# x's first two blocks in halves on both DMA queues, the gate weights on GpSimd's queue, and one warming product less, in a gated pair of linear-attention blocks

## The chip, the cores and the metric

The kernel runs on one core of a Trainium2 chip. The metric is the device time of one execution in microseconds (us); lower is better. A run gives one such time, and a kernel is judged by the median of its runs. One execution was also taken by the hardware profiler; its page and trace give times from the start of the span, in us unless marked ns.

The engines are TensorE (PE for its matrix products, PEld for its weight loads), VectorE (DVE), ScalarE (ACT), GpSimd (POOL) and SyncE (SP). A transfer is issued by an engine's queue (SPq, ACTq); the data are moved by 16 DMA engines that all queues share.

## What is computed

Two linear-attention blocks, A and B, work on the same x (2048 rows of 640, bf16) with weights of their own, and a sigmoid gate mixes them:

```
g = sigmoid((x * gate_w).sum(-1))
q, k, v = split of x @ wqkv, 32 heads of 20
phi(t) = where(t > 0, t + 1, exp(t)) + 1e-6
kv = sum over rows of phi(k) v^T;  z = sum over rows of phi(k)
o = phi(q) kv / (phi(q) z + 1e-6);  a = o @ wo
out = g * a_A + (1 - g) * a_B
```

A_x alone is used as x; B_x is not read.

## The kernel before

Everything stays in SBUF for the whole run. The contraction over 640 is done in five slices of 128 (DT = 5), the 2048 rows in 16 chunks of 128 (ST = 16), four chunks to a stretch of 512 (NB = 4, CB = 4). xT holds x transposed, xn holds it as it is; wk, wq and wv hold the slices of the weights.

*The loads of the start* (lines 151 to 173). The first 512 rows of x come as four blocks of 128 rows (load_x, line 152: 128 partitions of 1280 bytes, 160 KB; block q holds every fourth row). SP's queue issues block 0, slice 0 of A's key weights (load_wk, line 155, 160 KB), the gate weights g5 (line 161, five rows of 256 bytes), slice 2 of the key weights and slices 3 and 4 in one. ACT's queue issues block 1, slice 1 of the key weights, block 2, block 3, and then loads ACT's table of functions (line 165). After that SP issues A's query weights in three transfers (line 169) and 15 transposing loads (line 172), which bring the other three stretches of 512 rows into xT, five slices to a stretch. The framework gives the transfers of these two queues semaphores in turn, and a transfer that reuses one waits for the transfer that had it.

*GpSimd* builds constants: the identity `ident` (two instructions from masks.py, needed by the transpositions below), then maskE, I4, spread, E4 and an fp32 identity, which are read later.

*Warming products* (lines 208 and 209). Before x is there TensorE multiplies constants: six products of 512 columns and one of 256, whose result is not read.

*The first products* (k_first, lines 316 to 341, in an order written out by hand). x_transpose (lines 247 to 253) transposes a block of x by five TensorE products with the identity into PSUM, and VectorE copies them to xT in two pieces. gate_column (lines 220 to 225) transposes the gate weights in the same way, and ACT copies them as column 641 behind the key weights, so that the product for the second half of k (321 columns instead of 320) also yields the gate's sum. The order on TensorE is: the transpositions of blocks 0 and 1; the gate's transposition; eight products of k for blocks 0 and 1 with slices 0 and 1 (line 295, first the halves of 320 columns, then those of 321); the transpositions of block 2; four products with slice 2; the transpositions of block 3; the rest of k for blocks 0 to 3. After that come q for the first 512 rows, k for chunks 4 to 7 (these read the transposing loads' first stretch), and so on.

*The rest* (from line 947, an order written out by hand inside `tc.manual_schedule()`). k and q of both blocks, the sums over rows and the products with wv and wo follow, many of them in Strassen's form, with PSUM banks handed on from stage to stage. At lines 959 to 962 SP issues three loads, which bring the other three stretches of x into xn (640 KB each); A's wv and wo follow on the same queue. The first reader of these rows of xn is x_sum on VectorE (line 698).

Of the kernel before, what the change touches and what calls it, by code (L numbers as in the profile page):

```python
# [9 lines left out]
P = 128  # L10
# [9 lines left out]
NB = 4  # L20
CB = 4
HB = 512
# [6 lines left out]
RB = 256  # L29
# [4 lines left out]
def kernel(  # L34
# [11 lines left out]
    nc = tc.nc  # L46
    x2 = A_x.flatten_outer_dims()
# [44 lines left out]
    xn = persist.tile([P, ST, D], BF16, name="xn")  # L92
# [17 lines left out]
    g5 = persist.tile([DT, P], BF16, name="g5")  # L110
# [35 lines left out]
    xb0 = x2[0:CB * P, :].rearrange("(p q) d -> p q d", q=CB)  # L146
# [4 lines left out]
    def load_x(eng, lo, hi):  # L151
        eng.dma_start(out=xn[:, lo:hi, :], in_=xb0[:, lo:hi, :])

    def load_wk(eng, lo, hi):
        eng.dma_start(out=wk[0][:, lo:hi, 0:D], in_=wq_dram[0][:, lo:hi, D:2 * D])

    load_x(nc.sync, 0, 1)
    load_x(nc.scalar, 1, 2)
    load_wk(nc.sync, 0, 1)
    load_wk(nc.scalar, 1, 2)  # L160
    nc.sync.dma_start(out=g5[:], in_=gate_w.rearrange("(c p) -> c p", p=P))
    load_x(nc.scalar, 2, 3)
    load_wk(nc.sync, 2, 3)
    load_x(nc.scalar, 3, 4)
# [5 lines left out]
    for n in range(1, NB):  # L170
        for c in range(DT):
            nc.sync.dma_start_transpose(
                out=xT[:, c, n * HB:(n + 1) * HB], in_=x2[n * HB:(n + 1) * HB, c * P:(c + 1) * P]
# [4 lines left out]
    for r in range(4):  # L178
        rows = slice(32 * r, 32 * r + 32)
        nc.gpsimd.tensor_copy(out=I4[rows], in_=ident[rows, rows])  # L180
    nc.gpsimd.tensor_copy(
        out=spread[:].rearrange("p (h t) -> p h t", t=TW), in_=I4[:, :, None].to_broadcast([P, H, TW])
    )
    nc.gpsimd.memset(maskE[:], 1.0)
    for lo in range(0, HF, K6):
        part = maskE[:, lo:min(lo + K6, HF)]
        for sign, base in ((1, 0), (-1, Dh - 1)):
            nc.gpsimd.affine_select(
                out=part, in_=part, pattern=[[-sign * Dh, part.shape[1] // Dh], [0, Dh]],
# [3 lines left out]
    for rows, n in ((slice(0, 2 * H), H // 2), (slice(2 * H, P), H)):  # L193
        nc.gpsimd.tensor_copy(
            out=E4_rows[rows, 0:n], in_=I4[rows, 0:n, None].to_broadcast([rows.stop - rows.start, n, Dh])
# [9 lines left out]
    warm_raw = ps_raw("warm", 0)  # L205
    warm = banks(warm_raw)
    one_l, one_r = [nc.const_aps.tensor(1.0, [P, n], BF16) for n in (P, HB)]
    for n in [HB] * 6 + [RB]:
        nc.tensor.matmul(warm[:, 0, 0:n], lhsT=one_l, rhs=one_r[:, 0:n], start=True, stop=True)

    def by_group(dst, lhsT, src):
# [97 lines left out]
    def k_chunk(b, i, slot=None, lifted=False, between=None):  # L309
        pt = ps(f"k{'AB'[b]}", slot)  # L310
        for hf in range(2):
            for c in range(DT):
                k_mm(b, i, c, pt, hf)
        k_done(b, i, pt, lifted, between)
# [632 lines left out]
    with tc.manual_schedule():  # L947
# [8 lines left out]
        early = [(lambda k: lambda: sq_sum(k, 1))(k) for k in range(2, 5)] + [None, None]  # L956
        for i in range(hc, ST - 3):
            k_chunk(0, i, None, i in (8, 9, 11, 12), early[i - hc])
        for n in range(1, NB):
            nc.sync.dma_start(  # L960
                out=xn[:, n * CB:(n + 1) * CB, :], in_=x2[n * HB:(n + 1) * HB, :].rearrange("(q p) d -> p q d", p=P)
            )
        wv[0] = load_w(0, "v", nc.sync)
        load_wo(0, nc.sync)
# [161 lines left out]
        for i in range(1, half):  # L1126
            p, after = pairs[i], pairs[i + 1] if i + 1 < half else None
# [5 lines left out]
            q = after if i + 2 < half else p if after is None else None  # L1133
# [43 lines left out]
```

## Time and profile before

| | |
|---|---|
| median of 3 runs | 183.40 us |
| lowest, highest | 183.33, 183.84 us |
| the profiled execution's own time | 183.47 us |
| its span in the trace | 181.8 us |
| around the span | 1.7 us |
| busy: PE, PEld, DVE, ACT, POOL | 177.5, 118.8, 148.2, 108.2, 5.5 us |
| instructions | 3375 |

A row of the timeline gives the start, the length, the engine, the line, the operation with output and inputs, how many were merged into the row, and in brackets how long the engine sat idle before it and what ended that. "SPq" and "ACTq" are the queues' own issues: their length is the time for which the issue held the queue, and not the time of the transfer. A row of the DMA view gives what was loaded, by which queue, how many such transfers, their size, and the median time from issue to landing. A row of the windows view gives, for a stretch, its length and each engine's busy time with its count of instructions, then TensorE's clock as the profile has it, the DMA engines' busy share, and GB/s. The chain of waits follows the work that ended last back from the end; each of its rows is a start, a length and what took that time.

### The profile page before, as it was taken

To read this page: it belongs to the slowest core of one execution; us is meant where nothing else is said; L and a number is where in the kernel's file an instruction comes from. 1 tells how busy PE (TensorE), PEld (TensorE's weight loads), DVE (VectorE), ACT (ScalarE), POOL (GpSimd) and SP (SyncE) were. 2 spreads that over 40 slices of the span, in tenths; PEclk is the share of its full clock that TensorE was granted. 3 is DMA by queue.
4 is the path that set the end of the run, shared out by engine and by line. 5 is a ranking of instruction groups with operands and counts; after the bars stand their busy time and mean duration, and the time that the engine had idled before them with its cause. 6 is when DMAs were issued, how large, how long until landed. Compare 5 with 4: busy or idle time off the path is not lost.

```text
span 181.8 us, 3375 instructions
## 1 busy us (share of the span) xinstructions
PE 177.5 (98%) x1275; PEld 118.8 (65%) x1285; DVE 148.2 (82%) x267; ACT 108.2 (60%) x210; POOL 5.5 (3%) x23
## 2 busy tenths in 40 slices
PE   7999999999999999999999999999999999999993
PEld 3766656655666677676666665766678777777772
DVE  0478988999999796799898987997988988686764
ACT  2066579976884512785868696964814755466210
POOL 8300000000000000000000000000000000000000
PEclk9999999999999999999999999999999999999999
DMA  5996449984108133005000000053901470222132
GB/s 180 290 177 82 98 103 272 362 176 132 51 4 235 65 116 119 0 0 180 4 2 0 0 4 2 8 149 79 291 17 28 158 180 0 108 88 97 72 130 90
DMA packets 21519, 18.85 MB, mean 104 GB/s; under 512 B 9183, under 2 KB 20991, under 8 KB 21503
## 3 DMA queue, kind: packets, MB, share of 16 engines
q1 hardware_dynamic: 20638, 17.82, 36.1%
q10 hardware_dynamic: 864, 0.82, 1.5%
q8 instruction: 10, 0.16, 0.4%
q14 instruction: 7, 0.05, 0.1%
HBM read 11.86 MB, written 4.80 MB: 92 GB/s over the span
## 4 chain that ended last, share of the span: by engine, by line
PE 96%; DMA 2%; DVE 1%; issue 0%
PE gs L515 17%; PE kA L295 12%; PE kB L295 12%; PE q L413 11%; PE qA L348 7%; PE oy L762 6%; PE oz L762 5%; PE ox L762 4%; PE ow L762 4%; PE q L348 2%; PE gB L485 2%; PE gA L485 2%; DMA xn<-in_A_x_dram 2%; PE qB L348 1%; PE xt L250 1%; PE mA L645 1%
## 5 line engine op out<-in xcount | busy, mean ns | idle before, releaser
L295 PEld LDWEIGHTS <-xT 128*128 128x128 bf16 x320 | 31.1, 98 | 15.0 <-DVE xT L253 0.2
L272 DVE TENSOR_SCALAR e<-e 128x640 bf16<-128x640 bf16 (+2 forms) x58 | 19.6, 339 | 5.8 <-ACT e L264 5.2
L295 PE MATMUL kB<-wkB,xT 128*128 128x320 bf16 x160 | 24.2, 299 | 0.0
L295 PE MATMUL kA<-wkA,xT 128*128 128x320 bf16 (+1 forms) x160 | 23.4, 301 | 0.1
L264 ACT ACTIVATE e<-q 128x512 bf16<-128x512 f32 x26 | 15.7, 603 | 5.0 <-PE q L413 3.9
L515 PEld LDWEIGHTS <-xn 128*128 128x128 bf16 x128 | 12.2, 98 | 6.0 <-issue 1.3
L264 ACT ACTIVATE e<-kB 128x640 bf16<-128x640 f32 x16 | 11.4, 710 | 7.5 <-PE kB L295 7.3
L264 ACT ACTIVATE e<-kA 128x640 bf16<-128x640 f32 x16 | 11.3, 713 | 7.6 <-PE kA L295 7.5
L348 PE MATMUL qA<-xT,wqA 128*128 128x512 bf16 x57 | 13.3, 379 | 0.2
L348 PEld LDWEIGHTS <-wqA 128*128 128x128 bf16 x64 | 7.5, 117 | 5.9
L283 DVE SCALAR_TENSOR_TENSOR pk<-kB,e 128x640 bf16<-128x640 f32 x12 | 9.9, 823 | 1.0
L825 ACT COPY u<-ox 128x320 f32<-128x320 f32 x8 | 3.4, 425 | 11.4 <-PE ox L762 11.4
L762 PEld LDWEIGHTS <-xT 128*128 128x128 bf16 x85 | 8.1, 98 | 2.9
L762 PEld LDWEIGHTS <-pqTA 128*128 128x128 bf16 x85 | 8.1, 98 | 2.8
L767 DVE TENSOR_TENSOR osb<-oz,u 128x320 bf16<-128x320 f32 (+2 forms) x18 | 8.0, 454 | 2.2 <-PE oz L762 1.8
L762 PEld LDWEIGHTS <-pqTB 128*128 128x128 bf16 x80 | 7.8, 98 | 3.0
L515 PE MATMUL gs<-pk,xn 128*128 128x320 bf16 x64 | 9.4, 299 | 0.0
L283 DVE SCALAR_TENSOR_TENSOR pk<-kA,e 128x640 bf16<-128x640 f32 x10 | 8.2, 823 | 0.9
L431 DVE TENSOR_TENSOR q<-q,p 128x512 f32<-128x512 f32 x12 | 8.3, 692 | 0.8 <-PE q L413 0.6
L264 ACT ACTIVATE e<-qA 128x1024 bf16<-128x1024 f32 x6 | 6.2, 1027 | 4.2 <-PE qA L348 3.9
L485 PEld LDWEIGHTS <-xn 128*128 128x128 bf16 x64 | 6.3, 98 | 3.0
L515 PEld LDWEIGHTS <-S 128*128 128x128 bf16 x64 | 6.0, 98 | 2.5 <-issue 0.3
(187 smaller groups left out, 348.2 us busy)
## 6 DMA issues: line engine op xcount, KB each, us to landing
out_dram<-osb SPq DMA_DIRECT2D x14, 160.0 KB, 1.8
xn<-in_A_x_dram SPq DMA_DIRECT2D x3, 640.0 KB, 5.7
wvA<-in_A_wqkv_dram SPq DMA_DIRECT2D x1, 800.0 KB, 10.5
wkB<-in_B_wqkv_dram SPq DMA_DIRECT2D x1, 800.0 KB, 4.7
wqB<-in_B_wqkv_dram SPq DMA_DIRECT2D x1, 800.0 KB, 6.4
wvB<-in_B_wqkv_dram SPq DMA_DIRECT2D x1, 800.0 KB, 4.7
MA<-m_rows SPq DMA_DIRECT2D x1, 800.0 KB, 5.1
MB<-m_rows SPq DMA_DIRECT2D x2, 400.0 KB, 4.2
```

The costliest lines, as they stand in the source:

```text
L264: nc.scalar.activation(out=to, in_=part, func=ACT.Exp)
L272: nc.vector.tensor_scalar(self.e, self.e, 1.0, EPS, op0=ALU.min, op1=ALU.add)
L283: nc.vector.scalar_tensor_tensor(out=dst, in0=src, scalar=1.0 + EPS, in1=e, op0=ALU.add, op1=ALU.max)
L295: nc.tensor.matmul(pt[:, hf, 0:n], lhsT=xT[:, c, i * P:(i + 1) * P], rhs=wk[b][:, c, hf * HF:hf * HF + n], start=(c == 0), stop=(c == DT - 1),
L348: nc.tensor.matmul(dst, lhsT=mixed(wq[b][:, c, :], m), rhs=xT[:, c, n * HB:(n + 1) * HB], start=first, stop=last,)
L413: nc.tensor.matmul(dst, lhsT=left(c), rhs=right(c), start=first and k == 0, stop=k == len(cs) - 1, skip_group_check=not first,)
L431: nc.vector.tensor_tensor(out=dst, in0=src, in1=sb, op=ALU.add)
L485: nc.tensor.matmul(pt[:, hf, 0:HF], lhsT=xn[:, i, c * P:(c + 1) * P], rhs=pk[:, i, hf * HF:(hf + 1) * HF], start=(i == 0), stop=(i == ST - 1),
L515: nc.tensor.matmul(pt[:, n, 0:HF], lhsT=left[:, i, n * P:(n + 1) * P], rhs=right[:, i, :], start=(first and i == 0), stop=(i == hc - 1), s ...
L762: nc.tensor.matmul(dst, lhsT=left[:, c, r0:r0 + P], rhs=right[:, c, :], start=(first and c == 0), stop=(c == DT - 1), skip_group_check=not ...
L767: nc.vector.tensor_tensor(out=dst, in0=acc, in1=sb, op=ALU.add)
L825: nc.scalar.copy(out=self.u2[:], in_=self.at("x"))
```

## The change

Blocks 0 and 1 of x are each split by partitions: SP's queue loads partitions 0 to 63 and ACT's queue partitions 64 to 127, first of block 0, then of block 1. The key weights' slices follow on both queues as before. The gate weights leave SP's queue and become GpSimd's first transfer, the only one that GpSimd issues in this kernel. One of the six warming products of 512 columns is left out. In the later stage the three loads of x become two, one of 1280 KB and one of 640 KB.

```diff
-    load_x(nc.sync, 0, 1)
-    load_x(nc.scalar, 1, 2)
+    nc.gpsimd.dma_start(out=g5[:], in_=gate_w.rearrange("(c p) -> c p", p=P))
+    for i in range(2):
+        for eng, rows in ((nc.sync, slice(0, P // 2)), (nc.scalar, slice(P // 2, P))):
+            eng.dma_start(out=xn[rows, i], in_=xb0[rows, i])
     load_wk(nc.sync, 0, 1)
     load_wk(nc.scalar, 1, 2)
-    nc.sync.dma_start(out=g5[:], in_=gate_w.rearrange("(c p) -> c p", p=P))
     load_x(nc.scalar, 2, 3)
     load_wk(nc.sync, 2, 3)
     load_x(nc.scalar, 3, 4)
...
-    for n in [HB] * 6 + [RB]:
+    for n in [HB] * 5 + [RB]:
         nc.tensor.matmul(warm[:, 0, 0:n], lhsT=one_l, rhs=one_r[:, 0:n], start=True, stop=True)
...
-        for n in range(1, NB):
+        for lo, hi in ((1, 3), (3, NB)):
             nc.sync.dma_start(
-                out=xn[:, n * CB:(n + 1) * CB, :], in_=x2[n * HB:(n + 1) * HB, :].rearrange("(q p) d -> p q d", p=P)
+                out=xn[:, lo * CB:hi * CB, :], in_=x2[lo * HB:hi * HB, :].rearrange("(q p) d -> p q d", p=P)
             )
```

## The prediction

> **What bounds the kernel now.** I read the page first, then the chain of work that ended last, then the timeline of the first 8 us, then the DMA landings of that stretch.
>
> ```profile
> PE   7999999999999999999999999999999999999993
> PE 96%; DMA 2%; DVE 1%; issue 0%
> ```
>
> ```profile
> 0.81 3.06 DMA xn<-in_A_x_dram
> 3.87 0.05 issue
> 3.92 1.25 PE xt L250 x10
> ...
> 7.87 3.84 PE kA L295 x28
> ...
> 178.31 0.98 DVE osb L767 x3
> ```
>
> TensorE is busy in every slice but the first and last, and the chain says the same: from 3.92 us to the last additions it is a row of products. The only wait of size on it is the load of x's first block (issued 0.81, landed 3.87). So this change can only gain where it lets products start earlier, and what is gained at 4 us reaches the end only if no later wait eats it.
>
> ```profile
> 0.80 0.39 ACTq L152 DMA_DIRECT2D xn<-in_A_x_dram  x1
> ...
> 0.81 0.40 SPq L152 DMA_DIRECT2D xn<-in_A_x_dram  x1
> 0.84 2.93 PE L209 MATMUL warm<-const-bfloat16-1.0 128*128 128x512 bf16 x7 [0.84 <-PEq L1161]
> ...
> 1.22 0.46 ACTq L155 DMA_DIRECT2D wkA<-in_A_wqkv_dram  x1
> 1.26 0.44 SPq L155 DMA_DIRECT2D wkA<-in_A_wqkv_dram  x1
> 1.34 0.29 POOL masks.py:199 TENSOR_SCALAR_AFFINE_SELECT ident<-ident 128x128 bf16<-128x128 bf16 x1
> ...
> 1.71 0.94 ACTq L152 DMA_DIRECT2D xn<-in_A_x_dram  x2
> 1.75 0.37 SPq L161 DMA_DIRECT2D g<-in_gate_w_dram  x1
> ...
> 2.17 1.91 SPq L155 DMA_DIRECT2D wkA<-in_A_wqkv_dram  x2
> ...
> 2.67 1.28 ACT L165 ACT_TABLE_LOAD   x1 [2.67 <-issue]
> ...
> 3.91 0.98 PEld L250 LDWEIGHTS <-xn 128*128 128x128 bf16 x10 [0.83 <-DMA xn<-in_A_x_dram]
> ...
> 5.09 0.10 PEld L223 LDWEIGHTS <-g 5*128 5x128 bf16 x1 [0.20 <-issue]
> ...
> 5.21 1.55 PE L295 MATMUL kA<-wkA,xT 128*128 128x320 bf16 x8
> 5.32 0.30 ACT L225 COPY wkA<-warm 128x1 bf16<-128x1 bf16 x3 [1.36 <-PE warm L223]
> ...
> 6.60 0.44 PE L250 MATMUL xt<-ident,xn 128*128 128x128 bf16 x5
> ...
> 7.29 0.40 PEld L250 LDWEIGHTS <-xn 128*128 128x128 bf16 x5
> ```
>
> ```profile
> 2.93 0.84 PE L209 MATMUL warm<-const-bfloat16-1.0 128*128 128x512 bf16 x2
> ```
>
> Two things are to be seen. First, the start runs at half pace. Five warming products of 512 columns take from 0.84 to 2.93, 0.42 each, so 320 columns would take 0.26 and 128 columns 0.105; the 28 products of 320 columns from 7.87 on take 3.84, 0.137 each. The eight products between 5.21 and 6.60 take 1.39: with n at half pace, 0.26n + 0.137(8 - n) = 1.39 gives n = 2.4, so the pace doubles at 5.21 + 2.4 x 0.26 = 5.83. The clock row and the windows print full clock throughout; the spacing decides. Second, behind the first block the products are back to back.
>
> **The change part by part.** The landings, from issue:
>
> ```profile
> xn<-in_A_x_dram ACTq DMA_DIRECT2D x1, 160.0 KB, 2.9
> xn<-in_A_x_dram SPq DMA_DIRECT2D x1, 160.0 KB, 3.1
> ...
> wkA<-in_A_wqkv_dram ACTq DMA_DIRECT2D x1, 160.0 KB, 3.3
> wkA<-in_A_wqkv_dram SPq DMA_DIRECT2D x1, 160.0 KB, 3.4
> ...
> xn<-in_A_x_dram ACTq DMA_DIRECT2D x1, 160.0 KB, 3.6
> ...
> wkA<-in_A_wqkv_dram SPq DMA_DIRECT2D x1, 160.0 KB, 4.3
> ...
> xn<-in_A_x_dram ACTq DMA_DIRECT2D x1, 160.0 KB, 4.4
> ```
>
> ```profile
> 1.80:2.60 0.80, 0.80 (x4) 0.24 (x2) 0.00 (x0) 0.00 (x0) 0.73 (x4) 1.00 0.81 189
> 1.80:3.20 1.40, 1.40 (x5) 0.44 (x3) 0.00 (x0) 0.53 (x1) 1.21 (x7) 1.00 0.90 242
> ```
>
> *x in halves.* The last column is GB/s: 151 KB have moved by 2.60 and 339 KB by 3.20. Blocks 0 and 1 (164 KB each, side by side) are through at about 3.17 and landed at 3.87. With both queues on block 0, its 164 KB are through at about 2.64, 0.53 earlier, so it lands at 3.34. TensorE takes the 0.05 of the chain's issue, and I add 0.05 as it now waits for two DMAs: first transposition at 3.44 instead of 3.92. Bounds: no gain (3.87 stays), and 3.15, where the shortened warming frees the array. I take 3.44, since the rate comes from these very transfers.
>
> *One warming product less.* The last, of 256 columns, starts at 2.94 instead of 3.36 and streams 0.21: free at 3.15, so warming does not delay the transpositions. Left in, it would hold them to 3.57 and cost 0.13 of the gain.
>
> *Block 1* has the same bytes ahead of it as before, so 3.87; its transpositions are due at 3.44 + 5 x 0.105 = 3.97. No wait. Vector's copies out of PSUM follow the transpositions and come as much earlier; they are not on the chain.
>
> *Key weights.* Each queue issues one transfer more ahead of them: row 0 of the weights at about 1.70 instead of 1.26 (SP), row 1 at 1.66 instead of 1.22 (ACT), block 2 at about 2.15 instead of 1.71; SP's third is unchanged at 2.17, as the gate weights leave. The bytes ahead in each queue are the same and data began 1.0 after the first issue, so 2.7 at the earliest, while x still fills the queues till 3.17. I keep the landings: row 0 at 1.26 + 3.4 = 4.66, first product due at 5.21 - 0.48 = 4.73; row 2 at 2.17 + 4.3 = 6.47; block 2 at 1.71 + 3.6 = 5.31. Bounds for row 0: 4.66, and 0.44 later with the issue (0.37 lost at the first product, 0.19 at the end).
>
> *Gate weights by GpSimd.* SP saves 0.37. GpSimd issues the load ahead of the instructions that make the identity (ready at 1.34 + 0.29 = 1.63, wanted 3.44: it may hold the queue 1.8). The trace has no DMA of GpSimd. Issue: 0.37 (SP's row) to 1.3 (half of the 2.56 quoted below); either is covered. Landing: 2.9 to 5.7 after 0.80 (first row above, 640 KB row below); wanted at 4.61, so free up to 3.75. I take 3.0, the rows nearest in time, and nothing.
>
> *A wait moves.* SP's ninth load was held back:
>
> ```profile
> SPq L155 <- DMA xn<-in_A_x_dram: 1.2, 1, 1.2
> ```
>
> It waited for a first load, eight back. Now the ninth on the two queues is probably x's block 3 on ACT: issued when block 0 has landed, 3.35 instead of 2.19. Behind it on ACT stands the table load (1.28, now to about 5.1), then the three gate copies (0.30), done near 5.45; the first product that reads them is the fifth, at 5.8. Block 3 lands at 3.35 + 2.9 = 6.25 to 3.35 + 4.4 = 7.75; its weights load is due at 7.29 - 0.25 = 7.04. I take 6.7, as it queues behind block 2, which lands at 5.31 either way. SP's weights follow block 0 too, 0.3 earlier than before.
>
> *Three loads of x in two*, at 26.7:
>
> ```profile
> 26.68 1.68 SPq L960 DMA_DIRECT2D xn<-in_A_x_dram  x3
> ...
> xn<-in_A_x_dram SPq DMA_DIRECT2D x3, 640.0 KB, 5.7
> ...
> 36.63 0.69 DVE L698 TENSOR_TENSOR S<-xn 128x1024 bf16<-128x1024 bf16 x1
> ```
>
> The last lands near 27.9 + 6 = 34, the first reader is at 36.6: covered by 2.6. One issue (0.5) less on SP there, with nothing waiting.
>
> *The sum.* First product of k at 4.73; to 5.83 there is room for 1.10 / 0.26 = 4.2 at half pace, the other 3.8 take 0.52: the third block's transpositions start at 6.35 instead of 6.60. Half of the 0.48 is lost since the earlier products run at half pace: gain 0.25. What is late next: weights row 2 (6.47, wanted 6.63), block 3 (6.7, wanted 7.04), and the last transposing load of the second 512 rows:
>
> ```profile
> 9.90 2.56 SPq L172 DMA_TRANSPOSE xT<-in_A_x_dram  x2
> ...
> DMA to landing us min/median/max: 4.0/4.4/4.8
> ...
> 16.14 0.23 PEld L295 LDWEIGHTS <-xT 128*128 128x128 bf16 x2
> ```
>
> Its issue at 11.2 and 4.8 give 16.0; the second of the weight loads quoted, at 16.27, needs it. With 0.25 gained it is wanted at 16.02: just in time, and SP's row moves up by 0.3. So 183.47 - 0.25 = 183.22 for the profiled execution; the median of the runs, 183.40, lies 0.07 lower: **183.2**.
>
> A page speaks against the halves. The Trainium skill ("SBUF — State Buffer", sections "Door 1: The DMA port swizzle" and "Can I just issue two DMAs to hit both halves?") says that a transfer to 64 partitions reaches 8 of 16 ports, 196 GB/s, and that two on the two halves give only 6% more. By that estimate, 208 GB/s, block 1 and row 0 come 0.2 later and the time is 183.3. No run here shows it yet.
>
> **The rivals.**
>
> *B, more than forecast:* x lands as warming ends, and the double pace comes earlier too. Then 0.48 to 0.77 is kept, 182.6 to 182.9, say 182.8. For it: rates climb from 189 GB/s to over 300. Against it: weights row 0 (4.66) and row 2 (6.47) would have to land earlier too.
>
> *C, the data are no faster:* the two queues stay at the 189 GB/s of the first 0.8 us. 328 KB then take 1.73, to 3.53, 0.36 later; row 0 at 5.02, first product at 5.07, gain 0.14 / 2 = 0.07, so 183.33. Block 3 at its upper bound, 7.75 against 7.22, costs 0.5 more. 183.3 to 183.8, say 183.6.
>
> *D, slower, the pace:* the doubling came 5.0 after the first warming product. If the shorter warming makes that count start again with the transpositions, it comes at 3.44 + 5.0 = 8.43, 2.6 later, at half pace a loss of 1.3: 183.15 + 1.3 = **184.5**. It decides if the pause after warming (3.15 to 3.44) is long enough to undo it. Against it: the pause now, 3.57 to 3.92, is longer and undid nothing, else the doubling would stand at 8.9.
> The Trainium skill ("TensorE: Matmul & The Clock Gate", "Part 1: The HAM clock gate") has the same cause: full clock after one busy window of about 3.4 us, free-running. A missed window would cost 1.7 by that estimate.
>
> *E, slower, GpSimd:* the gate's transposition stands ahead of all products. If its load takes 5.7, it lands at 6.5; first product at 6.67, eight at full pace to 7.77 against 6.60, 1.17 later than before: 183.40 + 1.17 = **184.6**. It costs from 3.75 on and makes the kernel slower by 0.3% from 5.1 on.
>
> **How the numbers follow.** Forecast 0.41 (183.2), B 0.27 (182.8), C 0.12 (183.6), D 0.11 (184.5), E 0.09 (184.6). The range 182.6 to 184.0 takes in A's, B's and C's ends and leaves out D and E, 0.20. 0.3%, 0.55 us, is about what a measurement of this kernel can tell from no change. Faster by more: B but 0.02, and 0.01 of the forecast, 0.26. Slower: D, E and 0.02 of C, 0.22. Within: 0.52.
>
> **What the profile would show.** The first transposition at 3.4 to 3.5; block 1's without a gap; first product of k near 4.7; third transpositions near 6.35; the doubling still near 5.8; no wait before the products at 16. Wrong: a gap before the gate's weight load (E), half pace beyond 6 (D), an ACT queue held by block 3 with TensorE waiting near 7 (C), or the doubling well before 5.8 (B).

## The result: slower by 0.9%

| | before | after |
|---|---|---|
| median, 8 runs each | 183.63 us | 185.07 us |
| lowest, highest | 183.33, 183.88 us | 184.56, 186.32 us |
| ratio of after to before | | 1.0089 [1.007, 1.0108] |
| the profiled execution's own time | 183.47 us | 184.56 us |
| its span | 181.8 us | 182.8 us |

The forecast was 183.2 us, with 184.0 as the upper end of its range. The changed kernel is slower by 1.44 us in the median, and the profiled execution happens to be the fastest of its runs. Of all runs in this document one, of 188.51 us, counts as slow (over 1.5% above the fastest of its kernel) and is left out of that kernel's median and ratio.

From the page of the changed kernel: TensorE's row of the 40 slices and the shares of the chain by engine.

```profile
PE   7799999999999999999999999999999999999993
...
PE 93%; DMA 4%; DVE 1%; issue 0%
```

The second slice is no longer full, and DMA's share of the chain has doubled from 2% to 4%. The chain of waits says which transfers these are (start, length, what):

```profile
0.81 2.67 DMA xn<-in_A_x_dram
...
3.51 4.89 DMA xn<-in_A_x_dram
...
8.45 0.45 PE xt L251 x5
8.90 3.84 PE kA L296 x28
12.73 0.43 PE qA L349 x2
```

Block 0's halves are there at 3.48, earlier than the 3.87 of before. But then block 3, issued at 3.51, lands only at 8.40, and the fourth block's transpositions wait for it. Before, they stood at 7.59 and the products of q at 11.71:

```profile
7.59 0.28 PE xt L250 x5
...
11.71 0.22 PE qA L348
```

Now they stand at 8.45 and 12.73, the latter 1.02 later. The span is longer by the same 1.0, so all of this execution's loss lies ahead of 12.7 us.

TensorE's own rows of the timeline show three more waits ahead of that one (in brackets the idle time and what ended it):

```profile
3.53 0.71 PE L251 MATMUL xt<-ident,xn 128*128 128x128 bf16 x5 [0.18 <-DMA xn<-in_A_x_dram]
5.08 0.45 PE L251 MATMUL xt<-ident,xn 128*128 128x128 bf16 x5 [0.84 <-DMA xn<-in_A_x_dram]
5.47 0.17 PE L224 MATMUL warm<-ident,g 5*128 5x5 bf16 x1
...
6.27 1.11 PE L296 MATMUL kA<-wkA,xT 128*128 128x320 bf16 x7 [0.38 <-DMA wkA<-in_A_wqkv_dram]
...
8.45 0.45 PE L251 MATMUL xt<-ident,xn 128*128 128x128 bf16 x5 [0.24 <-DMA xn<-in_A_x_dram]
```

Block 1, which now needs both queues' second halves, makes TensorE wait 0.84. Slice 1 of the key weights makes it wait 0.38. From 6.27 on seven products (1.11), five transpositions (0.28) and four products (0.55) would bring the fourth block to 8.21, 0.62 later than the 7.59 of before; block 3 adds the rest of the 1.02, 0.24 as a wait and 0.17 because five transpositions right behind this wait take 0.45 on the chain and not 0.28.

The queues' issues of the same execution, with "x2" and "x3" for issues merged into one row:

```profile
0.81 1.20 SPq L160 DMA_DIRECT2D xn<-in_A_x_dram  x2
0.81 1.38 ACTq L160 DMA_DIRECT2D xn<-in_A_x_dram  x2
...
1.29 0.64 POOL L157 DMA_DIRECT2D g<-in_gate_w_dram  x1 [0.78 <-POOLq L1162]
...
2.06 1.58 SPq L155 DMA_DIRECT2D wkA<-in_A_wqkv_dram  x3
2.23 0.69 ACTq L155 DMA_DIRECT2D wkA<-in_A_wqkv_dram  x1
...
2.96 0.93 ACTq L152 DMA_DIRECT2D xn<-in_A_x_dram  x2
```

Each half holds its queue 0.57 to 0.78 us (two in 1.20 on SP and in 1.38 on ACT), where a whole block held it 0.39 to 0.40. Slice 0 is therefore issued at 2.06 instead of 1.26, slice 1 at 2.23 instead of 1.22, block 2 at 2.96 instead of 1.71. From issue to landing slice 1 then takes 4.0, against 3.3 before, and blocks 2 and 3 take 4.4 in the median (block 3 alone 4.89, against 4.4 before):

```profile
xn<-in_A_x_dram ACTq DMA_DIRECT2D x2, 160.0 KB, 4.4
...
wkA<-in_A_wqkv_dram ACTq DMA_DIRECT2D x1, 160.0 KB, 4.0
g<-in_gate_w_dram POOLq DMA_DIRECT2D x1, 1.2 KB, 2.4
```

Slice 1 lands at 2.23 + 4.0 = 6.23. Slices 3 and 4 of the key weights (320 KB) go out at 3.24, 0.27 ahead of block 3, where in the kernel before they went out at 3.69, well behind it. The gate weights land at 1.29 + 2.4 = 3.7, well ahead of 5.47, where they are read.

### The profile page after: what moved, and what is told of

Its sections match the earlier page's. It is cut to its first block, busy times and chain, and to the rows that moved or that the text cites. A ratio compares the mean times of both kernels' runs of the same rounds, so it can differ in the third digit from the quotient of the medians.

```text
span 182.8 us, 3387 instructions
## 1 busy us (share of the span) xinstructions
PE 177.5 (97%) x1284; PEld 118.2 (65%) x1284; DVE 148.2 (81%) x267; ACT 108.2 (59%) x210; POOL 6.1 (3%) x24
## 4 chain that ended last, share of the span: by engine, by line
PE 93%; DMA 4%; DVE 1%; issue 0%
PE gs L516 17%; PE kB L296 12%; PE q L414 11%; PE kA L296 11%; PE qA L349 7%; PE oy L763 6%; PE oz L763 5%; PE ox L763 4%; DMA xn<-in_A_x_dram 4%; PE ow L763 4%; PE q L349 3%; PE gB L486 2%; PE gA L486 2%; PE qB L349 1%; PE mA L646 1%; PE kvA L630 1%
```

## The experiments

Two theories stood against each other. **Data:** the halves push the later transfers back, and TensorE waits for them. **Pace** (the prediction's rival D): TensorE's half pace lasts longer. The first two groups of kernels below are mostly about the data, the third about the pace, the fourth about what was then open. None of them was faster than the kernel before. In each section the time is the median with the lowest and the highest, and the ratio is to the kernel before, timed beside it on the same chip (medians of 183.26 to 183.35 us).

### One part at a time

**The halves alone**, in the kernel before:

```diff
-    load_x(nc.sync, 0, 1)
-    load_x(nc.scalar, 1, 2)
+    for i in range(2):
+        for eng, rows in ((nc.sync, slice(0, P // 2)), (nc.scalar, slice(P // 2, P))):
+            eng.dma_start(out=xn[rows, i], in_=xb0[rows, i])
```

> The kernel before with blocks 0 and 1 in halves alone (gate weights stay on SP, seven warming products, three loads of x later). Theory S (splitting: a half holds its queue as long as a whole block or longer, so everything behind it is issued 0.8 to 1.0 us later): 184.6 to 185.1, block 1 lands near 5.0, first product with slice 1 of the key weights near 6.2, each half's issue about 0.57. Theory G (GpSimd's transfer holds up the other two queues): 183.2 to 183.5, issues of 0.40, block 1 near 3.9. Theory W (the shorter warming delays the doubling of the pace): 183.2 to 183.6.

Measured: 184.86 us (184.25 to 185.22), ratio 1.008 [1.0061, 1.01]. The halves alone make nearly the whole loss. In this execution the pace had doubled by 4.91 (five transpositions there take 0.45), so what it loses it loses to late data. Here ten transfers stand ahead of slices 3 and 4, which are held back until a half of block 1 has landed at 4.87; the chain goes through them:

```profile
1.40 3.46 DMA xn<-in_A_x_dram
...
4.88 4.27 DMA wkA<-in_A_wqkv_dram
```

**The gate weights alone** to GpSimd's queue (their line moved up, `nc.sync` to `nc.gpsimd`):

```diff
+    nc.gpsimd.dma_start(out=g5[:], in_=gate_w.rearrange("(c p) -> c p", p=P))
     load_x(nc.sync, 0, 1)
...
-    nc.sync.dma_start(out=g5[:], in_=gate_w.rearrange("(c p) -> c p", p=P))
```

> The kernel before with the gate weights on GpSimd's queue alone. Theory S: 183.3 to 183.8, no difference; issues of SP and ACT stay near 0.40 to 0.45. Theory G: 184.3 to 185.0; issues of SP and ACT grow to 0.58 or more while GpSimd issues, block 1 of x lands a full microsecond later than 3.7. Theory W: no difference.

Measured: 184.09 us (183.66 to 185.19), ratio 1.0047 [1.0028, 1.0065]. The forecast had put this load at nothing. The timeline shows SP's three issues of key weights back to back, and TensorE waiting for block 2:

```profile
1.27 1.37 SPq L155 DMA_DIRECT2D wkA<-in_A_wqkv_dram  x3
```

```profile
7.55 0.45 PE L250 MATMUL xt<-ident,xn 128*128 128x128 bf16 x5 [1.19 <-DMA xn<-in_A_x_dram]
```

With one transfer fewer on the two queues, slices 3 and 4 (320 KB) are the eighth and no longer held back; they go out near 2.2 instead of 3.69, when block 2, which is wanted first, is still under way. Not all of block 2's lateness is seen to come from sharing: in this execution fifteen of the 16 DMA engines had done their part of it at 6.11 and the last at 7.50 (before, 5.17 and 5.36). Why one engine falls behind is not shown.

**The gate weights by GpSimd, and a copy of that load by SP** in the old place, which nothing reads: the hold is back.

```diff
+    nc.gpsimd.dma_start(out=g5[:], in_=gate_w.rearrange("(c p) -> c p", p=P))
...
-    nc.sync.dma_start(out=g5[:], in_=gate_w.rearrange("(c p) -> c p", p=P))
+    nc.sync.dma_start(out=g5b[:], in_=gate_w.rearrange("(c p) -> c p", p=P))
```

> The kernel before with the gate weights loaded by GpSimd and used from there, and a second, unread copy of them loaded by SP in the old place, so that SP and ACT have as many transfers as before and the key weights' slices 3 and 4 are again held till x has landed (issue near 3.6; in the run with the gate weights on GpSimd alone they went out at 2.20 and block 2 landed at 7.5). Theory H (what costs is the hold that is lost: 320 KB of key weights go out 1.5 us early and share the engines with block 2, block 3 and slice 2): 183.2 to 183.5, block 2 lands near 5.4. Theory G (GpSimd's transfer itself slows one or more DMA engines): 184.0 to 184.4, block 2 near 6 to 7.5.

Measured: 183.48 us (182.9 to 184.1), ratio 0.9999 [0.9979, 1.0019].

```profile
2.15 1.99 SPq L156 DMA_DIRECT2D wkA<-in_A_wqkv_dram  x2
```

The two issues take 1.99 together, so the second waits again. GpSimd's transfer costs nothing by itself; what the kernel before has in SP's tiny load is a hold on the large one behind it.

**One warming product less**, alone:

```diff
-    for n in [HB] * 6 + [RB]:
+    for n in [HB] * 5 + [RB]:
```

> The kernel before with one warming product of 512 columns less. Theories S and G: 183.5 to 183.8, no difference, since x lands at 3.87 either way. Theory W: 184.2 to 185.2 in the median, with the products between 5.2 and 9 at half pace in those executions that take longest.

Measured: 183.33 us (182.9 to 183.96), ratio 1.0003 [0.9989, 1.0017]. No difference, with the data of before.

**The three later loads of x as two**, alone (the last part of the change's diff):

> The kernel before with only the three later loads of x as two (1280 KB and 640 KB). Theory: covered by over 2 us, so no difference within 0.3%: 183.2 to 183.6. Rival: the larger load takes DMA engines from A's wv and wo, and a product waits beyond 36 us; then 0.3 us or more is lost and the chain of waits shows it.

Measured: 183.55 us (183.03 to 183.75), ratio 1.0006 [0.9992, 1.0021]. No difference, as the prediction had it.

**The changed kernel with the gate weights back on SP's queue**, behind slices 0 and 1:

```diff
-    nc.gpsimd.dma_start(out=g5[:], in_=gate_w.rearrange("(c p) -> c p", p=P))
...
+    nc.sync.dma_start(out=g5[:], in_=gate_w.rearrange("(c p) -> c p", p=P))
```

> The changed kernel with the gate weights back on SP's queue behind slice 0 of the key weights. Theory S: 184.6 to 185.2, as the changed kernel. Theory G: 183.2 to 183.6. Theory W: 184.6 to 185.2, but with issues of 0.40 and block 1 landing near 3.9.

Measured: 185.41 us (184.39 to 185.83), ratio 1.0104 [1.0078, 1.013]; the interval overlaps that of the changed kernel. Its profile showed something else, taken up below under the pace:

```profile
5.45 2.32 PE L296 MATMUL kA<-wkA,xT 128*128 128x320 bf16 x8
```

Eight products of k take 2.32, where seven of them took 1.11 in the changed kernel's first profile.

### What about a half costs

**Halves by columns**, 128 partitions of 640 bytes, instead of 64 partitions of 1280, in the kernel before:

```diff
-    load_x(nc.sync, 0, 1)
-    load_x(nc.scalar, 1, 2)
+    for i in range(2):
+        for eng, cols in ((nc.sync, slice(0, HF)), (nc.scalar, slice(HF, D))):
+            eng.dma_start(out=xn[:, i, cols], in_=xb0[:, i, cols])
```

> The kernel before with blocks 0 and 1 in halves by columns: every half has all 128 partitions, 640 bytes each, and is issued by the same queues in the same order as in the halves by partitions. Theory P (a transfer to 64 partitions is what holds a queue for 0.57 to 0.87): issues near 0.40, block 1 lands near 4.1, 183.2 to 183.8. Theory N (the number of transfers ahead counts, whatever their shape): issues of 0.57 and more again, block 1 near 4.8, 184.6 to 185.1.

Measured: 184.55 us (183.8 to 186.06), ratio 1.0067 [1.004, 1.0094].

```profile
0.80 0.91 ACTq L159 DMA_DIRECT2D xn<-in_A_x_dram  x2
...
0.81 0.88 SPq L159 DMA_DIRECT2D xn<-in_A_x_dram  x2
```

```profile
6.09 1.28 PE L296 MATMUL kA<-wkA,xT 128*128 128x320 bf16 x8 [0.85 <-DMA wkA<-in_A_wqkv_dram]
```

Two halves now hold a queue 0.88 to 0.91 together, so it is the 64 partitions that made it 1.20 and more. Yet the time gains little: a half is still one transfer more ahead of slice 0 (issued at 1.73 instead of 1.26), and TensorE waits for that slice until 6.09. Here too one engine is behind: fifteen had done their part of slice 0 at 5.08 and the last at 6.05, where all 16 had done theirs by 4.70 before. The intervals of halves by partitions and by columns overlap.

**Each block on its own queue**, both of its halves by partitions there:

```diff
-    load_x(nc.sync, 0, 1)
-    load_x(nc.scalar, 1, 2)
+    for rows in (slice(0, P // 2), slice(P // 2, P)):
+        for i, eng in ((0, nc.sync), (1, nc.scalar)):
+            eng.dma_start(out=xn[rows, i], in_=xb0[rows, i])
```

> The kernel before with block 0 in two halves by partitions, both on SP, and block 1 in two, both on ACT: the bytes stand in each queue as before, only cut in two. Theories P and N: issues of 0.57 and more, key weights' slice 0 issued near 2.05 as with the halves on both queues, 184.5 to 185.0. A third theory, O (the two queues write the two halves of one block at the same time and get in each other's way): issues near 0.45, 183.3 to 183.8.

Measured: 185.31 us (184.21 to 186.16), ratio 1.009 [1.0054, 1.0126]. So that the halves of one block go through both queues is not what costs. Its profile is of the slowest run (186.16) and also shows seven products of k at half pace, 2.03.

**The gate weights one place up on SP's queue**, so that slice 0 alone is issued 0.4 later, with whole blocks and the same eight transfers:

```diff
+    nc.sync.dma_start(out=g5[:], in_=gate_w.rearrange("(c p) -> c p", p=P))
     load_wk(nc.sync, 0, 1)
     load_wk(nc.scalar, 1, 2)
-    nc.sync.dma_start(out=g5[:], in_=gate_w.rearrange("(c p) -> c p", p=P))
```

> The kernel before with the gate weights' load moved one place up on SP's queue, ahead of key-weight slice 0: the same eight transfers and the same queue, only slice 0 issued about 0.4 us later (1.65 instead of 1.26), slice 2 unchanged. Theory I (a later issue means a later landing): slice 0 lands 0.2 to 0.4 later, near 5.0, just under the 5.21 where the first product of k stands now, so 183.3 to 183.6. Rival K (the prediction's step: the bytes ahead set the landing, not the issue): slice 0 lands near 4.7 as before, and no difference.

Measured: 184.12 us (183.22 to 185.9), ratio 1.0047 [1.0022, 1.0073].

```profile
1.67 4.45 DMA wkA<-in_A_wqkv_dram
...
6.16 1.25 PE kA L295 x8
```

This is the prediction's disputed step nearly by itself; the 1.2 KB of the gate weights now also stand ahead of slice 0. Slice 0, issued at 1.67, takes 4.45 to land and not 3.4, and TensorE waits until 6.16 for it. In that execution fifteen of the 16 DMA engines had done their part of it at 5.06 and the last at 6.12. Rival K, that the bytes ahead set the landing and not the issue, is out: even the fifteen are 0.36 later than the whole slice was before (4.70), about as much as the issue. My own size (0.2 to 0.4 later) fits them, and the last engine adds 1.06 that no theory here had; whether the later issue brings that about is not shown.

### The pace

**The changed kernel with eight warming products of 512 columns** instead of five:

```diff
-    for n in [HB] * 5 + [RB]:
+    for n in [HB] * 8 + [RB]:
```

> The changed kernel with three warming products of 512 columns more, so that warming lasts to about 4.6 and fills the pause before block 1 lands near 5.0. If the doubling of the pace, put off by the pauses, is a part of the loss: 184.2 to 184.7 in the median and a spread below 1 us. If the loss is the data's alone: 184.9 to 185.3, spread as in the changed kernel (184.56 to 186.32).

Measured: 185.04 us (184.91 to 185.7), ratio 1.0084 [1.0057, 1.011]. The median stays, the spread narrows from 1.8 to 0.8.

```profile
5.50 1.45 PE L296 MATMUL kA<-wkA,xT 128*128 128x320 bf16 x8
7.86 0.45 PE L251 MATMUL xt<-ident,xn 128*128 128x128 bf16 x5 [0.92 <-DMA xn<-in_A_x_dram]
```

The pace doubles within the first eight products, and TensorE still waits 0.92 for block 2. So in this execution late data alone hold the kernel near 185.

**A try at a better kernel: block 0 alone in halves by columns.** Block 1 stays whole, slices 0 and 1 follow on SP's queue, the gate weights go by GpSimd, five warming products; eight transfers on the two queues, as before.

```diff
-    load_x(nc.sync, 0, 1)
+    nc.gpsimd.dma_start(out=g5[:], in_=gate_w.rearrange("(c p) -> c p", p=P))
+    for eng, cols in ((nc.sync, slice(0, HF)), (nc.scalar, slice(HF, D))):
+        eng.dma_start(out=xn[:, 0, cols], in_=xb0[:, 0, cols])
+    load_wk(nc.sync, 0, 1)
     load_x(nc.scalar, 1, 2)
-    load_wk(nc.sync, 0, 1)
-    load_wk(nc.scalar, 1, 2)
-    nc.sync.dma_start(out=g5[:], in_=gate_w.rearrange("(c p) -> c p", p=P))
+    load_wk(nc.sync, 1, 2)
...
-    for n in [HB] * 6 + [RB]:
+    for n in [HB] * 5 + [RB]:
```

> Block 0 alone in two halves by columns (128 partitions of 640 bytes), one on each queue; block 1 whole on ACT's queue behind its half; key-weight slices 0 and 1 on SP's queue behind its half; the gate weights on GpSimd's queue; five warming products of 512 columns. Eight transfers stand ahead of slices 3 and 4 on the two queues, as in the kernel before, and each should hold its queue 0.40 to 0.48 us. Theory I (issue times and the hold set the landings): block 0 lands near 3.2 us and slices 3 and 4 stay held till then; slice 0 is issued at 1.25 as before and lands near 4.7, slice 1 (issued 1.7 instead of 1.22) near 5.0, block 2 near 5.3; the first product of k near 4.8 instead of 5.21 and a median 0.2 to 0.4 us under the kernel before, about 183.0. Rival S (a half of any shape at the head of the queues leaves engines behind and the weights late, as in the run with four halves by columns): slice 0 or 1 lands at 6 us and the time is 184 or more.

Measured: 185.19 us (183.31 to 185.83), ratio 1.0071 [1.004, 1.0102]. The twelve runs fall apart: five took 183.31 to 184.10, seven 185.18 to 185.83. The profile is of the fastest, 183.31:

```profile
5.40 1.11 PE L296 MATMUL kA<-wkA,xT 128*128 128x320 bf16 x7 [0.29 <-DMA wkA<-in_A_wqkv_dram]
6.35 0.44 PE L251 MATMUL xt<-ident,xn 128*128 128x128 bf16 x5
```

Here the third block's transpositions stand at 6.35, just where the forecast had them for the change (6.60 before). But that shows no gain: the kernel before, timed beside it, has a median of 183.30, and in two other profiles with blocks 0 and 1 whole the same transpositions stand at 6.28 (one warming product less) and 5.99 (the merged loads alone). What the seven slower runs lack is either data or pace. The next two kernels change only the warming products, so the data keep their order.

**The same with eight warming products of 512 columns:**

> The kernel with block 0 alone in halves by columns (185.19 median, 183.31 to 185.83) with three warming products of 512 columns more (eight): warming lasts to about 4.4 us, past the landing of block 1 (4.26), so TensorE has no pause of over 0.3 us up to the first product of k. Theory D (the pause after warming lets the half pace last one period longer in some executions): the runs above 185 vanish, 183.3 to 183.8 in all. Rival L (in those runs the data are late): the runs above 185 stay, median near 185.

Measured: 183.63 us (183.32 to 184.56), ratio 1.0022 [1.0007, 1.0037].

```profile
5.75 1.51 PE L296 MATMUL kA<-wkA,xT 128*128 128x320 bf16 x8
```

The first product of k starts only at 5.75, but without a wait, and the pace doubles within the eight (1.51). No run is above 184.56.

**The same with three:**

> The kernel with block 0 alone in halves by columns with only three warming products of 512 columns (and the one of 256): warming ends near 2.3 us and TensorE is idle for 1 us more before block 0 lands at 3.3. Theory D: nearly all runs, not seven of twelve, are above 185, and the profile shows the products of k between 5 and 8 us at 0.26 each. Rival L: the same mixture as with five warming products, median 184 to 185.3.

Measured: 185.41 us (184.76 to 186.27), ratio 1.0118 [1.0089, 1.0146].

```profile
4.54 0.71 PE L251 MATMUL xt<-ident,xn 128*128 128x128 bf16 x5 [0.82 <-DMA xn<-in_A_x_dram]
...
5.30 2.32 PE L296 MATMUL kA<-wkA,xT 128*128 128x320 bf16 x8
...
9.02 0.74 PE L251 MATMUL xt<-ident,xn 128*128 128x128 bf16 x5
```

The first product of k starts earlier than in the kernel with eight (5.30 against 5.75), and yet the time is 1.8 us longer: eight products take 2.32, and five transpositions at 9.02 still take 0.74, half pace. With 183.63, 185.19 and 185.41 for eight, five and three warming products, theory D holds in this order of loads.

**The kernel before with three warming products:**

```diff
-    for n in [HB] * 6 + [RB]:
+    for n in [HB] * 3 + [RB]:
```

> The kernel before with three warming products of 512 columns instead of six; the data are untouched. TensorE is idle from about 2.3 to 3.9 us. Theory D: a pause of this length costs a period in most executions, 184.5 to 186. Rival (the pace comes from the work behind the first transposition alone): no difference, 183.2 to 183.6. With five warming products there was none.

Measured: 184.26 us (184.11 to 184.75), ratio 1.006 [1.0042, 1.0079], between the two expectations.

```profile
3.73 1.25 PE L250 MATMUL xt<-ident,xn 128*128 128x128 bf16 x10 [1.23 <-DMA xn<-in_A_x_dram]
...
5.03 2.32 PE L295 MATMUL kA<-wkA,xT 128*128 128x320 bf16 x8
```

A pause of 1.23 ahead of the transpositions costs 1.0 even where the data are untouched; with five warming products, in whose profile the transpositions follow within 0.15, there was no cost.

**The changed kernel with column halves, five and eight warming products:**

> The changed kernel with its four halves by columns (128 partitions of 640 bytes) instead of by partitions. Theory I: the halves hold their queues 0.40 to 0.48 us instead of 0.57 to 0.78, so slice 0 is issued near 1.7 instead of 2.06, block 3 near 3.2 instead of 3.5; about half of the loss comes back: 184.0 to 184.6, against 185.07. Rival S (four halves of any shape cost the same, by their number): 184.9 or more.

Measured: 185.41 us (184.95 to 185.79), ratio 1.0107 [1.0087, 1.0128]. Rival S was right: the shape of the halves does not help the time. It does help block 1: its halves by columns land at 3.49 and 3.67, by partitions at 4.17 and 5.04, and here all ten transpositions run without a wait. The wait is now for the slices: slice 0, issued at 1.74, lands at 5.63, later than the 5.35 of the changed kernel, which issued it at 2.06. So the issue alone does not set the landing either.

```profile
5.68 2.30 PE L296 MATMUL kA<-wkA,xT 128*128 128x320 bf16 x8 [1.15 <-DMA wkA<-in_A_wqkv_dram]
```

> The changed kernel with all four halves by columns (185.41, 184.95 to 185.79; doubling near 9.1 in its profile) with eight warming products of 512 columns instead of five. Data as there: key-weight slice 1 lands near 5.8, so the first products of k come 0.6 later than before. Theory D: the doubling comes by 6.6 and the time falls to what the late data cost, 183.7 to 184.3. Rival L: no change, 185.2 or more.

Measured: 184.84 us (184.16 to 185.43), ratio 1.0082 [1.0058, 1.0105], between the two expectations.

```profile
6.16 1.28 PE L296 MATMUL kA<-wkA,xT 128*128 128x320 bf16 x8 [0.34 <-DMA wkA<-in_A_wqkv_dram]
...
8.72 0.45 PE L251 MATMUL xt<-ident,xn 128*128 128x128 bf16 x5 [0.45 <-DMA xn<-in_A_x_dram]
```

The eight products are back at 1.28 instead of 2.30, and the median is 0.57 lower. What stays are waits for slices and for block 3, again the ninth transfer of the two queues. The kernel with block 0 alone in halves and the same eight warming products has 183.63: this order of loads with both blocks in halves costs 1.2 us more.

### What was left open

**Block 3 by GpSimd's queue** in the changed kernel, behind the identity:

```diff
-    load_x(nc.scalar, 3, 4)
...
     make_identity(nc, ident[:])
+    load_x(nc.gpsimd, 3, 4)
```

> The changed kernel with block 3 of x loaded by GpSimd's queue, behind the two instructions that make the identity: eight transfers stand ahead of slices 3 and 4 on the two queues again, and block 3 isn't held. Issue near 2.8 to 3.4 instead of 3.51, landing 6.5 to 7.5 instead of 8.40. Theory: the wait for block 3 goes (0.4 in the profile), the key weights' lateness stays (0.6): 184.4 to 184.8. Rival: slice 1 or slices 3 and 4 become as late, or GpSimd's transfer of 128 partitions is slow, and the median stays at 185.0 or above.

Measured: 185.66 us (184.19 to 186.57), ratio 1.0125 [1.0084, 1.0165]. The theory missed in the median. Block 3 does come early, issued at 2.12 and landed at 5.76, and TensorE no longer waits for it, but slice 1 is nearly as late as in the changed kernel (6.08), and in the profiled execution (185.66) the products run at half pace:

```profile
6.12 2.03 PE L296 MATMUL kA<-wkA,xT 128*128 128x320 bf16 x7 [0.15 <-DMA wkA<-in_A_wqkv_dram]
```

Its fastest run, 184.19, lies 0.4 under the changed kernel's fastest, but that is one run, and the kernel before was 0.28 faster beside it too (183.35 against 183.63). Whether the wait for block 3 is worth 0.4 by itself stays open.

**The changed kernel once more**, for a second profile:

> The changed kernel once more, for a second profile. If its time is above 185, theory D expects products of k at 0.26 each beyond 6 us; the rival expects full pace by then and a transfer that lands later than in the first profile. If its time is near 184.6, the profile should look like the first, with block 3 last.

Measured: 185.33 us, one run. It is the same kernel, and the timeline of TensorE shows the late doubling of theory D, and a later landing too:

```profile
3.52 0.71 PE L251 MATMUL xt<-ident,xn 128*128 128x128 bf16 x5 [0.17 <-DMA xn<-in_A_x_dram]
5.11 0.71 PE L251 MATMUL xt<-ident,xn 128*128 128x128 bf16 x5 [0.88 <-DMA xn<-in_A_x_dram]
...
5.87 2.32 PE L296 MATMUL kA<-wkA,xT 128*128 128x320 bf16 x8
...
8.06 0.45 PEld L251 LDWEIGHTS <-xn 128*128 128x128 bf16 x5 [0.46 <-DMA xn<-in_A_x_dram]
...
8.57 0.80 PE L296 MATMUL kA<-wkA,xT 128*128 128x320 bf16 x4
```

Its chain has the last 28 products of k at:

```profile
9.65 3.84 PE kA L296 x28
```

Up to the second five transpositions both executions have the same starts and waits within 0.04. In the first, these five took 0.45: the pace had doubled. In the second they take 0.71, eight products take 2.32, and full pace is there within the four products at 8.57 (0.80, where four at full pace take 0.71). The last 28 products of k start at 9.65 instead of 8.90, 0.75 later, and the time is 0.77 longer. But not all of this is the pace. TensorE's load of block 2 at 8.06 (PEld) ends a wait for it: block 2 landed at 8.02 here and at 6.89 in the first execution; block 3 landed at 8.97 instead of 8.40. With these landings and full pace the 28 products would have started near 8.06 + 0.45 + 0.55 + 0.28 = 9.34, by an estimate from the rows of the first execution. By it, 0.44 of the 0.75 is late data and 0.31 the pace.

## Why the prediction was wrong, point by point

**Block 0: near in this execution, in part by luck.** Forecast: landed at 3.34, first transposition at 3.44. Measured: 3.48 and 3.53, against 3.87 and 3.92 before. But in the six other profiles with whole blocks block 0 landed at 3.40 to 3.72, so the 3.87 from which the gain was counted was late, and what the halves gain is less than the 0.53 forecast.

**The step that failed: "Key weights ... I keep the landings".** The prediction put the slices' issues 0.44 later and let them land when they had landed before, since the bytes ahead in each queue were the same. Two things were wrong in it. The issue of a half was costed like that of a whole block, about 0.45, and takes about 0.6, so slices and block 2 go out 0.8 to 1.25 later and not 0.44. And the landings did not stay: with its issue moved by 0.4 and 1.2 KB ahead of it, slice 0 cost 0.8 us. In the changed kernel slice 0 lands at 5.35 instead of 4.70, and slice 1, which was not bounded at all, at 6.23, 1.8 later than before; slice 1 costs 0.62 of the profiled execution's 1.02. What sets a slice's landing is known only in part: fifteen engines come later by about the delay of the issue where only that was moved, one engine can come 1 us behind them, and the column halves show that an earlier issue need not land earlier.

**Block 1: wrong in the same way.** "the same bytes ahead of it as before, so 3.87 ... No wait." Its half on ACT's queue was issued at 1.42, where the whole block was issued at 0.80, and took 3.6 to land instead of 2.9; TensorE waits 0.84 until 5.08. This wait leaves no mark of its own in the sum, since slice 1 is later still.

**A wait moves: mechanism right, size wrong.** Block 3 became the ninth transfer, was held until block 0 had landed, and was issued at 3.51 (forecast 3.35). It landed at 8.40; the upper bound was 7.75, from 4.4 between issue and landing, and it took 4.89. Slices 3 and 4, 320 KB, had gone out 0.27 ahead of it; the prediction saw them come earlier and put no price on that. That they are the reason is not shown by itself. Block 3 adds 0.41 in the profiled execution. Rival C had this direction and at most 183.8, because it let the weights come in time.

**The pace: the doubling was taken as fixed near 5.8.** It is not fixed in one and the same kernel: between the two groups of five transpositions in one execution, near 8.7 in another. The record of TensorE's clock that the traces keep says the same: full clock from 4.58 in the first and from 8.75 in the second, and from 5.84 in the kernel before, where the prediction had worked out 5.83 from the lengths. Rival D had the mechanism with a chance of 0.11. That its price, 184.5, lies near the time is luck, since late data alone make the median. The argument against it, that a pause of 0.35 had undone nothing before, rested on one execution. Which pause brings a late doubling is not settled: in the kernel before it was one of 1.23 after three warming products; in the changed kernel the wait for block 1 stands in both profiles and the doubling was late in one, and with column halves, where that wait is gone, it was late too. The Trainium skill ("TensorE: Matmul & The Clock Gate", "Part 1: The HAM clock gate") says that the window of about 3.4 us is free-running and that the same kernel therefore doubles at different products in different runs. The two profiles agree, with doublings 4.2 us apart at equal starts, and the stretches of full clock in their records, 177.49 and 174.08 us, differ by 3.41. The prediction, which had cited the page, gave it too little weight.

**Gate weights by GpSimd: near in the change.** They landed at 3.7 (forecast 3.0), wanted at 5.47, and rival E did not occur. Alone, the move costs 0.8, through the hold and not through GpSimd; in the change the halves bring more transfers than the move takes away.

**One warming product less, three loads in two: right** for the data of before; neither makes a difference.

**The gain itself: not seen.** With block 0 alone in halves the fastest execution has the third transpositions at the forecast's 6.35, and 183.31 us, but the kernel before beside it had a median of 183.30. With eight warming products it took 183.63, ratio 1.0022 [1.0007, 1.0037]. No kernel here shows that an earlier block 0 shortens the time.

**The rule on the halves.** The windows of the two kernels (length, busy times, clock, DMA share, GB/s last), first after, then before:

```profile
1.80:2.60 0.80, 0.80 (x4) 0.24 (x3) 0.00 (x0) 0.00 (x0) 0.79 (x4) 1.00 0.37 83
2.60:3.40 0.80, 0.75 (x3) 0.06 (x1) 0.00 (x0) 0.00 (x0) 0.80 (x4) 1.00 0.84 244
3.40:4.20 0.80, 0.67 (x5) 0.45 (x5) 0.00 (x0) 0.28 (x1) 0.68 (x4) 1.00 0.87 192
```

```profile
2.60:3.40 0.80, 0.80 (x4) 0.20 (x2) 0.00 (x0) 0.73 (x1) 0.67 (x3) 1.00 0.97 315
3.40:4.20 0.80, 0.66 (x5) 0.29 (x4) 0.00 (x0) 0.56 (x1) 0.80 (x5) 1.00 1.04 365
```

While halves of 64 partitions are under way the two queues move 83 to 244 GB/s, against 189 to 365 before. The Trainium skill ("SBUF — State Buffer", sections "Door 1: The DMA port swizzle" and "Can I just issue two DMAs to hit both halves?") has two such halves at only 6% over one, by the prediction's estimate 208 GB/s. The mean of the three rows of after is 173, so the trace agrees in direction. The later issues are in these rows too and are not separated. Nor do the rates settle the time: column halves on all 128 partitions gave 185.41, no better than the 185.07, as they too stand ahead of the weights.

**The account.** The profiled execution loses 1.02 in the span to late data: slice 1 0.62, block 3 the rest. The second execution is 0.77 longer, by the estimate above more than half of it through still later data and the rest through a later doubling. Late data alone are enough for the median: with eight warming products, whose profile shows full pace early, the ratio is 1.0084, against 1.0089. The late doubling bears on single runs. How often the changed kernel doubles late was not measured beyond these two profiles, and no profile shows what made two of its eight runs take 186.12 and 186.32.

## What to carry to other kernels

Ahead of the first product, what counts is the last of the loads it needs. Splitting the first load made every later issue on the queue later here, and the weights behind it cost more than x gained. Count the transfers ahead of each load and the time that each issue holds the queue, and count also which transfer becomes the one that must wait for a semaphore to come free; taking a tiny load off a queue can cost more than it saves. A start that is shorter but has pauses can lose more to TensorE's half pace than it gains, so judge it by several executions and not by one profile. The same holds for the baseline: here the landing of block 0 before the change was taken from one execution in which it was late.

## What the runs showed of the hardware that was not expected

- The issue of a transfer of 64 partitions of 1280 bytes held SP's or ACT's queue 0.56 to 0.87 us, that of 128 partitions of 640 bytes 0.44 to 0.46 (0.88 and 0.91 for two), and that of 128 partitions of 1280 bytes mostly 0.35 to 0.47 (behind such halves up to 0.69).
- One DMA engine of the 16 can be about 1 us behind the other fifteen in one transfer: slice 0 at 5.06 and 6.12 with the gate weights moved up, at 5.08 and 6.05 with column halves, both with no transfer by GpSimd in the kernel. In the kernel before, slice 0 had 4.68 and 4.70. Why is open.
- In two executions of one kernel with the same starts to 0.04 us the pace doubled some 4 us apart, while the clock column of the windows showed 1.00 throughout; the lengths of the products tell, and so does the trace's clock record, which starts only at the doubling.
